# Remainder rows stacked by split half, and a masked broadcast of the running maximum by matmuls

## The chip, the cores and the metric

One core of a Trainium2 chip. The metric is the device time of one execution in microseconds, the median of several runs; lower is better.

## The reference

The input goes through three layers, all in 32-bit floats.

1. A recurrent attention (an mLSTM) over 2 batches, 8 heads, 768 positions and head size 40. With gates i and f, a running maximum m and a state C (40 x 40 per head):

```
m_new = max(f_t + m, i_t);  f_stab = exp(f_t + m - m_new);  i_stab = exp(i_t - m_new)
C = f_stab C + i_stab v_t k_t^T;   n = f_stab n + i_stab k_t
y_t = sigmoid(o_t) * (C q_t) / max(|n . q_t|, 1)
```

2. The 1536 tokens of 320 numbers are normalised (root mean square, times rms_g), then `silu(x w_gate) * (x w_val) @ w_out` with 1536 inner columns.
3. `leaky_relu(x w_in, 0.01) @ w_out` with 2048 inner columns.

## The kernel before, in words

**Attention.** The 768 positions are cut into 6 chunks of 128; chunk c of batch b is tile T = 2c + b, so there are 12 tiles. Within a tile the recurrence is written as a masked product: a cumulative sum Fl of f, a = i - Fl, and the running maximum A of a (both by scans on DVE over 16 rows, one per batch and head: `scan_f`, `scan_a`). The weight of position s for position t is exp(a_s - A_t) for s <= t. So each tile needs A_t as a row that all 128 partitions see. For tile 0 that is done by `first_a` (token `fa`): matmuls with one column of the identity, repeated 128 times, as weights and the 16 rows of A as moving data (L216), which leaves A in PSUM. For all other tiles A is stored to DRAM (`a_out`, L237) and loaded back to all 128 partitions (`ld_a`, token `da`, L274, 512 KB each). The causal mask adds 1e30 where s > t: on DVE inside `att_arg` for tiles 0 and 1 (L306, eight instructions per tile, then one wide exp per half on ACT, L310), on POOL for the rest (`att_mask`, L314), followed by four exps per half on ACT (L304). A half is the even or the odd heads (e = 0 or 1).

The further steps of a tile are `qk` (scores, L288), `p` (scores times weights, DVE), `av` (times v, by halves, L353), `inn` (product with the state of earlier chunks, L364), `k` and `kv` (keys times their weight, product for the state, L376), then the gating, the norm and `xn`, and `tp` (three transposes, L458). `xh` and `xl` write X, the normalised tokens with features on partitions, as two halves of a 32-bit number: the high half is what the format fp32r keeps, the low half is the rest.

**Weights.** Weights arrive as 64-bit floats and are turned into 32-bit ones by integer steps on DVE and ACT (`to_f32`), then split into high and low halves. The 320 features are 128 + 128 + 64. The main block of an up weight is token `a`; the 64 remaining rows of two blocks are loaded as one 128-partition block, token `r` (L523, L525), and their high and low halves are re-copied by DMA from SBUF to SBUF to both partition halves of their place, token `x` (`rest`, L531, two transfers of 128 KB per weight block).

**Up and down.** `up` forms each 128-column block in eight matmuls: high x high, high x low, low x high for the two full blocks, and for the 64 rows one matmul with the high weights and one with the low weights, in which partitions 64 to 127 of X hold the low half of the same 64 features. Token `U.g.f.h` is one such block (h = 0 gate, 1 value) of the second layer over a group of 3 or 4 tiles, `D` and `DW` its down products, `H` and `O` those of the third layer.

**Filling matmuls.** `busy` (token `id.1`, L182) multiplies constants of 512 columns in bf16; the result is not used. The order has 77 of them, 62 ahead of the first U and 15 behind it, of which six are at the very end.

**What sets the order.** The whole program is played from one string, ORDER: each token calls one function, and each engine executes its instructions in the order in which they were issued. All loads and stores are on the queue of SP, in that order too. Nothing is reordered later; an engine waits at an instruction until its data are there and its buffer is free.

Of the kernel before, what the change touches and what calls it, by code (L numbers as in the profile page):

```python
# [48 lines left out]
id.1 y2.0.0 co.1.1.2 a.0 cv.1.1.2 co.0.1.2 cv.0.1.2 qk.1 p.1.0 dc.1.2 co.0.2.6 dv.1.2 st.0 y2.0.1 y2.0.2 qk.2 da.2
mask.2.1 arg.2.1 p.1.1 k.2 r.1 id.1 dr.2.6 r.1 cb.0 a.0 dgb av.1.0 av.1.1 de.2 dE.2.6 wA.1 x.0 a.1 mask.2.0 a.2 xn.0  # L50
xc.0 a.1 a.1 x.1 id.1 dq.4 cv.0.2.6 a.2 id.1 tp.0 arg.2.0 abs.1 a.1 wR.2 y1.1 r.2 da.4 mask.4.0 id.1 id.1 rec.1 yr.1
a.2 wR.3 sq.1 id.1 a.2 r.2 xh.0 id.1 id.1 k.1 wA.3 a.3 kv.1 st.1 co.1.2.6 p.2.0 id.1 av.2.0 da.3 de.3 mask.3.0 arg.3.0
dq.3 r.2 p.2.1 av.2.1 xl.0 qk.3 cb.1 mask.3.1 id.1 eq.2 inn.2 cv.1.2.6 id.1 id.1 arg.3.1 wR.4 id.1 y2.1.0 y2.1.1
y2.1.2 a.3 r.2 a.3 id.1 x.2 id.1 id.1 xn.1 mask.4.1 wA.4 a.4 p.3.1 y1.2 dn.3 k.3 p.3.0 id.1 a.3 arg.4.1 abs.2 rec.2
qk.4 x.3 kv.2 id.1 de.4 eq.4 xc.1 tp.1 dn.4 arg.4.0 p.4.0 av.4.0 id.1 c.3 c.2 r.3 a.4 a.4 yr.2 eq.3 id.1 wA.5 da.5
mask.5.0 r.3 de.5 id.1 av.3.0 av.3.1 a.4 sq.2 y2.2.0 th.4 p.4.1 y2.2.1 r.3 dn.5 r.3 a.5 y2.2.2 xn.2 xc.2 id.1 mask.5.1
xh.1 id.1 id.1 inn.3 th.3 a.5 wR.5 abs.3 id.1 kv.3 y1.3 id.1 id.1 xl.1 tp.2 xh.2 xl.2 arg.5.0 id.1 dq.5 wA.6 qk.5
rec.3 yr.3 a.5 a.5 U.0.0.0 arg.5.1 b.0 a.6 eq.5 st.3 cb.3 p.5.0 p.5.1 k.5 T.0.0 E.0.0 sq.3 da.6 mask.6.1 dc.2.6 dv.2.6
b.0 a.6 b.0 b.0 U.0.0.1 av.4.1 dq.6 inn.4 a.6 abs.4 wB.1 av.5.0 mask.6.0 arg.6.0 c.5 y2.3.0 y2.3.1 qk.6 y2.3.2 U.0.1.0
T.0.1 y1.4 M.0.0 rec.4 yr.4 sq.4 dn.7 b.1 av.5.1 a.6 c.4 arg.6.1 k.4 kv.4 xn.3 id.1 xc.3 b.1 id.1 y2.4.0 y2.4.1 inn.5  # L60
kv.5 abs.5 x.6 wA.7 a.7 th.5 st.4 p.6.1 E.0.1 de.6 st.5 da.7 id.1 p.6.0 mask.7.0 wB.3 tp.3 xh.3 xl.3 S.0.0 dn.6 de.7
dq.7 wB.2 y1.5 U.0.1.1 U.0.2.0 a.7 b.1 L.0.0 a.7 a.7 mask.7.1 arg.7.1 eq.6 av.6.0 id.1 dq.8 av.6.1 rec.5 yr.5 sq.5 b.3
b.1 b.2 arg.7.0 T.0.2 y2.5.0 dn.10 b.3 id.1 id.1 id.1 b.3 M.0.1 y2.5.1 y2.4.2 xn.4 xc.4 y2.5.2 xn.5 xc.5 x.5 E.0.2 b.3
da.8 da.9 qk.7 id.1 p.7.0 U.0.2.1 S.0.1 L.0.1 tp.5 xh.5 xl.5 cb.4 th.7 c.6 wA.8 p.7.1 U.0.3.0 T.0.3 E.0.3 M.0.2 inn.6
qk.8 abs.6 tp.4 k.7 xh.4 xl.4 th.6 y1.6 wA.10 U.0.3.1 k.6 M.0.3 S.0.3 L.0.3 x.7 U.1.0.0 T.1.0 rec.6 U.1.1.0 E.1.0
S.0.2 yr.6 mask.8.0 arg.8.0 b.2 b.2 kv.6 st.6 mask.8.1 wB.5 b.5 L.0.2 b.2 b.5 b.5 cb.6 U.1.0.1 wB.4 M.1.0 T.1.1 E.1.1
D.0.0.0 K.0.0.0 mask.9.1 b.4 b.4 b.4 sq.6 U.1.1.1 M.1.1 b.4 wB.6 b.6 c.8 y2.6.0 dq.9 y2.6.1 p.8.0 b.6 b.5 U.1.2.1
U.1.2.0 D.0.0.1 cb.5 c.7 arg.8.1 y2.6.2 xn.6 S.1.1 D.0.0.2 b.6 xc.6 tp.6 xh.6 xl.6 av.7.0 p.8.1 wB.7 av.7.1 K.0.0.2
dn.8 k.8 av.8.0 id.1 L.1.1 de.8 av.8.1 T.1.2 eq.7 E.1.2 M.1.2 S.1.2 L.1.2 eq.8 x.4 b.6 th.8 r.4 r.4 r.4 wR.8 r.4 inn.8
y1.8 U.1.3.0 T.1.3 K.0.0.1 U.1.3.1 E.1.3 abs.8 M.1.3 wB.9 inn.7 kv.7 kv.8 S.1.0 b.7 da.10 abs.7 arg.9.1 qk.9 y1.7  # L70
U.0.5.1 b.7 L.1.0 dn.9 b.7 U.0.4.0 rec.8 yr.8 mask.9.0 de.9 S.1.3 L.1.3 D.1.0.2 T.0.4 E.0.4 b.7 arg.9.0 p.9.0 U.0.4.1
sq.8 mask.10.1 st.7 D.1.0.0 cb.7 c.9 p.9.1 r.5 k.9 K.1.0.0 K.1.0.2 M.0.4 S.0.4 L.0.4 U.0.5.0 T.0.5 E.0.5 av.9.0
D.1.0.1 M.0.5 S.0.5 mask.10.0 arg.10.0 L.0.5 U.0.6.0 T.0.6 E.0.6 y2.8.0 y2.8.1 y2.8.2 U.0.6.1 a.8 M.0.6 S.0.6 eq.9
# [757 lines left out]
```

## Time and profile before

| | |
|---|---|
| median of 3 runs | 491.5 us (490.97 to 492.52) |
| span of the profiled execution | 488.2 us |
| PE busy | 468.6 us (96%), 2785 matmuls |
| DVE, ACT, POOL busy | 282.5, 224.9, 62.8 us |
| moved by DMA | 51.10 MB |
| mean granted TensorE clock | 0.965 of full |

The span is from the first to the last instruction of the profiled execution; the page gives no other time for it. PE is TensorE's matmuls, PEclk the granted clock, of which 1.00 is 2.4 GHz and 0.50 is 1.2 GHz; a mean between them is a window with both. Matmuls are pipelined, so the length of one is more than its share of PE's time; a row that merges several gives the time of all.

### The profile page before, as it was taken

Reading aid. Unit: us, or ns where it says so; the run is one execution under the profiler, and the core shown is the slowest. Engines: PE = TensorE matmul, PEld = TensorE weight load, DVE = VectorE, ACT = ScalarE, POOL = GpSimd, SP = SyncE. Lnnn points to the kernel's source line nnn. Section 1 sums busy time; section 2 is a strip of 40 time slices with the busy share of each in tenths; the row PEclk is TensorE's granted clock in tenths of the full one; section 3 lists DMA queues with packets and bytes.
Section 4 is the critical chain, followed back from the end, with each engine's and each line's share of the span. In section 5 each row is a group of like instructions: output and inputs, shape, how many; then the busy total and the mean of one; then the engine's idle time right before and its main releaser. Section 6 shows DMA issues by size and latency. Waiting matters only on the chain.

```text
span 488.2 us, 7459 instructions
## 1 busy us (share of the span) xinstructions
PE 468.6 (96%) x2785; PEld 415.0 (85%) x2785; DVE 282.5 (58%) x618; ACT 224.9 (46%) x525; POOL 62.8 (13%) x82
## 2 busy tenths in 40 slices
PE   7959699899999998999999999999999999999998
PEld 4537589799999998999988888888898898988987
DVE  7776888877557676887767666654432121232232
ACT  2556366575533614655533444665434342532150
POOL 3325743513321200000000000000000000000000
PEclk7975869999999999999999999999999999999999
DMA  7899996963910011736430410232000000010101
GB/s 279 283 300 279 276 284 174 280 198 88 257 69 0 1 44 31 213 113 186 149 97 1 120 55 0 62 104 72 0 2 0 1 1 1 0 42 0 68 0 55
DMA packets 36868, 51.10 MB, mean 105 GB/s; under 512 B 2800, under 2 KB 26272, under 8 KB 36832
## 3 DMA queue, kind: packets, MB, share of 16 engines
q1 hardware_dynamic: 36832, 50.62, 35.7%
q8 instruction: 22, 0.36, 0.3%
q14 instruction: 14, 0.11, 0.1%
HBM read 43.31 MB, written 2.06 MB: 93 GB/s over the span
## 4 chain that ended last, share of the span: by engine, by line
PE 79%; DVE 8%; DMA 5%; issue 3%; ACT 2%; POOL 1%; SPq 1%; POOLq 0%; DVEq 0%; ACTq 0%
PE h L569 18%; PE g L569 13%; PE v L569 12%; PE xa L632 7%; PE oa L704 6%; PE oa L702 6%; PE oa L703 6%; PE xw L650 4%; PE o L353 2%; DMA Ab<-A_d 2%; DMA raw_A<-wgv 2%; PE s L288 1%; PE o L364 1%; DMA wA<-rest 1%; PE o L376 1%
## 5 line engine op out<-in xcount | busy, mean ns | idle before, releaser
L569 PE MATMUL h<-X,wA 128*128 128x512 f32 x384 | 93.0, 395 | 0.0
L569 PEld LDWEIGHTS h<-X,wA 128*128 128x128 f32 x384 | 71.4, 188 | 15.6
L614 DVE TENSOR_TENSOR sl<-u,sh 128x512 fp32r<-128x512 f32 x48 | 32.4, 690 | 85.3 <-ACT sh L608 85.3
L569 PE MATMUL g<-X,wA 128*128 128x384 f32 (+1 forms) x352 | 75.0, 359 | 0.0
L569 PE MATMUL v<-X,wA 128*128 128x384 f32 (+1 forms) x352 | 74.1, 356 | 0.6 <-DVE th L602 0.6
L569 PEld LDWEIGHTS g<-X,wA 128*128 128x128 f32 x352 | 63.5, 191 | 5.1 <-ACT wA L514 0.2
L569 PEld LDWEIGHTS v<-X,wA 128*128 128x128 f32 x352 | 62.3, 188 | 5.8 <-DVE th L602 0.9
L689 ACT ACTIVATE u<-h 128x512 f32<-128x512 f32 x48 | 28.2, 597 | 75.4 <-PE h L569 57.8
L704 PE MATMUL oa<-wB,sl 128*128 128x320 f32 x192 | 59.4, 309 | 0.0
L703 PE MATMUL oa<-wB,sh 128*128 128x320 f32 x192 | 59.3, 309 | 0.0
L702 PE MATMUL oa<-wB,sh 128*128 128x320 f32 x192 | 59.3, 309 | 0.0
L632 PE MATMUL xa<-sh,wB 128*128 128x384 f32 x160 | 46.2, 339 | 0.0
L608 ACT CAST sh<-th 128x384 fp32r<-128x384 f32 (+1 forms) x44 | 23.6, 541 | 46.8 <-DVE th L602 39.3
L703 PEld LDWEIGHTS oa<-wB,sh 128*128 128x128 f32 x192 | 36.0, 188 | 1.0
L702 PEld LDWEIGHTS oa<-wB,sh 128*128 128x128 f32 x192 | 36.0, 188 | 0.9
L704 PEld LDWEIGHTS oa<-wB,sl 128*128 128x128 f32 x192 | 36.0, 188 | 0.3 <-DVE sl L614 0.3
L591 ACT ACTIVATE th<-g 128x384 f32<-128x384 f32 (+1 forms) x44 | 22.7, 518 | 27.6 <-PE g L569 20.3
L598 DVE SCALAR_TENSOR_TENSOR th<-th,g 128x384 f32<-128x384 f32 (+1 forms) x44 | 25.7, 587 | 14.8 <-ACT th L591 14.2
L614 DVE TENSOR_TENSOR sl<-th,sh 128x384 fp32r<-128x384 f32 (+1 forms) x44 | 27.0, 617 | 12.2 <-ACT sh L608 11.9
L608 ACT CAST sh<-u 128x512 fp32r<-128x512 f32 x48 | 29.0, 620 | 9.4 <-PE oa L703 7.3
L632 PE MATMUL xa<-sl,wB 128*128 128x384 f32 x96 | 32.4, 338 | 0.0
L182 PE MATMUL busy<-const-bfloat16-1.0 128*128 128x512 bf16 x77 | 27.6, 477 | 4.1 <-DVE aeu L208 3.4
(113 smaller groups left out, 672.2 us busy)
## 6 DMA issues: line engine op xcount, KB each, us to landing
raw_B<-wo SPq DMA_DIRECT2D x28, 320.0 KB, 3.4
raw_A<-wgv SPq DMA_DIRECT2D x12, 512.0 KB, 6.1
qkt<-qk SPq DMA_DIRECT2D x12, 512.0 KB, 6.0
nat<-nat SPq DMA_DIRECT2D x12, 484.0 KB, 6.6
Ab<-A_d SPq DMA_DIRECT2D x11, 512.0 KB, 6.4
wA<-rest SPq DMA_DIRECT2D x40, 128.0 KB, 4.5
raw_A<-wi SPq DMA_DIRECT2D x8, 512.0 KB, 4.3
eb<-e_d SPq DMA_DIRECT2D x20, 128.0 KB, 6.4
```

Source lines behind the costliest of these rows:

```text
L182: PE.matmul(dst, idle[0], idle[1][:, 0:dst.shape[1]], start=start, stop=start)
L569: PE.matmul(dst, a, x, start=(i == 0), stop=(i == len(seq) - 1))
L591: A.activation(th, u[0], AF.Tanh, scale=0.5)
L598: V.scalar_tensor_tensor(out=u["t"], in0=u["t"], scalar=1.0, in1=u[0], op0=ALU.add, op1=ALU.mult)
L608: A.copy(u["h"], u["t"])
L614: V.tensor_tensor(u["l"], u["t"], u["h"].bitcast(F32), op=ALU.subtract)
L632: PE.matmul(xa, w, x, start=(k == 0), stop=(k == len(seq) - 1))
L650: PE.matmul(xas["w", g, i], a, x, start=(f == NE and k == 0), stop=(f == NF - 1 and k == len(seq) - 1),)
L689: A.activation(t, u[0], AF.Prelu, alpha=0.01)
L702: PE.matmul(dst, sh[:, ts], wb[:, 0:DM], start=first, stop=False)
L703: PE.matmul(dst, sh[:, ts], wb[:, DM:], start=False, stop=False)
L704: PE.matmul(dst, sl[:, ts], wb[:, 0:DM], start=False, stop=last)
```

## The change

Five things, and a new ORDER.

- **Remainder rows.** The place of the 64 remaining rows of a weight block is one column block of 128 partitions, high half on one side and low half on the other, written there by ACT and DVE directly. The re-copies (token `x`) are gone. X gets a sixth block, the low half of its third block; the two remainder matmuls of `up` use the stacked weights with the third and the sixth block.
- **Broadcast by matmuls.** `fa` is now called for both halves of tiles 0 to 3. One matmul of the identity with the mask (both in fp32r, 512 columns) starts the sum in PSUM, four matmuls add A. For these tiles ACT reads A from PSUM in four exps per half; the loads `da` and the masks on POOL for tiles 2 and 3 and the subtractions on DVE for tiles 0 and 1 are gone. The mask value is 2^100.
- **Gate rows** live in x2, which is not needed before the down products, and not in five of the eight places for up weights.
- Clearing of two tiles moves from DVE to POOL. The identity and the mask are loaded as one and copied to fp32r (token `cr`, ACT, twice in the order).
- The low part of X is one subtraction where it was two; A in DRAM is laid out by chunk, so that a broadcast reads 4 KB in one piece.

```diff
-        for j in range(4):
-            bh = 2 * j + e
-            PE.matmul(A0[e][:, j * L:(j + 1) * L], ident[0:16, bh:bh + 1].to_broadcast([16, 128]), A_[:, 0], start=True, stop=True)
+    def rows_a(T, e):
+        c, b = divmod(T, B)
+        pa = st_[T].setdefault("A", {})[e] = psum(f"A{T}_{e}", "acc" if b else "gv", 2)
+        PE.matmul(pa.rearrange("p (j l) -> p j l", j=4), ident_r, mask_r.unsqueeze(1).to_broadcast([128, 4, L]), start=True, stop=False)
+        for j in range(4):
+            bh = b * H + 2 * j + e
+            PE.matmul(
+                pa[:, j * L:(j + 1) * L], ident[0:16, bh:bh + 1].to_broadcast([16, 128]), A_[:, c], start=False, stop=j == 3,
+            )
...
-            if c > 0:
-                A.activation(w[:, j], t["Ab"][:, h], AF.Exp, scale=-1.0, bias=col)
...
+            src = t["A"][e][:, j * L:(j + 1) * L] if T < NPA else t["Ab"][:, h]
+            A.activation(w[:, j], src, AF.Exp, scale=-1.0, bias=col)
...
+        halves = [(up_weights(2 * i + e), slice(64 * e, 64 * e + 64), slice(64 - 64 * e, 128 - 64 * e)) for e in range(2)]
+        for w, hi, lo in halves:
+            A.copy(w[hi, 4], x[hi])
         yield
-        V.tensor_tensor(r[:, 1], x, r[:, 0].bitcast(F32), op=ALU.subtract)
+        for w, hi, lo in halves:
+            V.tensor_tensor(w[lo, 4], x[hi], w[hi, 4].bitcast(F32), op=ALU.subtract)
         yield
-
-    def rest(key):
-        r, lo, w = WR[key // 2], 64 * (key % 2), WA[key]
-        for i in range(2):
-            Q.dma_start(out=w[64 * i:64 * i + 64, :, 2].bitcast(F32), in_=r[lo:lo + 64].bitcast(F32))
...
-            (w[:, 0, 2, ms], X[:, 2, cs]), (w[:, 1, 2, ms], X[:, 2, cs]),
+            (w[:, 4, ms], X[:, 2, cs]), (w[:, 4, ms], X[:, 5, cs]),
```

The order is too long to show. PE's tokens up to the sixth U, without the fillers (which are in the order before alone):

```
before: co.0.0.1 fa.0 fa.1 qk.0 co.1.0.1 av.0.0 av.0.1 kv.0 co.1.1.2 co.0.1.2 qk.1 dc.1.2 co.0.2.6 qk.2 av.1.0 av.1.1
 tp.0 kv.1 co.1.2.6 av.2.0 av.2.1 qk.3 inn.2 qk.4 kv.2 tp.1 av.4.0 av.3.0 av.3.1 inn.3 kv.3 tp.2 qk.5 U.0.0.0 dc.2.6
 U.0.0.1 av.4.1 inn.4 av.5.0 qk.6 U.0.1.0 av.5.1 kv.4 inn.5 kv.5 tp.3 U.0.1.1 U.0.2.0 av.6.0 av.6.1 qk.7 U.0.2.1
after: co.0.0.1 fa.0.1 fa.1.1 co.0.1.2 fa.0.0 qk.0 fa.1.0 co.1.0.1 qk.1 co.0.2.6 av.0.0 av.0.1 fa.2.0 kv.0 av.1.0 av.1.1
 co.1.2.6 qk.2 fa.2.1 fa.3.1 co.1.1.2 kv.1 fa.3.0 av.2.0 qk.3 av.2.1 inn.2 av.3.0 av.3.1 inn.3 kv.3 qk.4 kv.2 tp.0 tp.1
 tp.2 dc.1.2 qk.5 U.0.1.0 U.0.0.0 U.0.1.1 av.4.0 av.4.1 inn.4 dc.2.6 av.5.0 av.5.1 inn.5 qk.6 kv.5 U.0.0.1 U.0.2.0
 U.0.2.1
```

(`co` transposes columns of gates, one per chunk; `dc` is the decay.) The loads issued ahead of the first U, as tokens times their size on the page:

```
before, to the load of tile 5's q and k: wA 6 x 512, wR 6 x 256, wB 1 x 320, q and k 6 x 512, nat 6 x 484, da 5 x 512,
 de 4 x 128 x 2, re-copies 4 x 128 x 2, small ones about 500 (KB)
after, to de of tile 4: wA 6 x 512, wR 4 x 256, wB 2 x 320, q and k 6 x 512, nat 5 x 484, da 3 x 512, de 4 x 128 x 2,
 small ones about 500 (KB)
```

## Rows read from the trace of the kernel before

**Rows 1.** The page, busy us (share of the span) and instructions per engine.

```profile
PE 468.6 (96%) x2785; PEld 415.0 (85%) x2785; DVE 282.5 (58%) x618; ACT 224.9 (46%) x525; POOL 62.8 (13%) x82
```

**Rows 2.** The page, the span in 40 slices, in tenths.

```profile
PEclk7975869999999999999999999999999999999999
DMA  7899996963910011736430410232000000010101
```

**Rows 3.** Windows, sum over 0 to 72 us: busy us (instructions) per engine.

```profile
sum 72.00, PE 57.80 PEld 41.27 DVE 54.76 ACT 35.74 POOL 30.90; mean PE 0.80 PEld 0.57 DVE 0.76 ACT 0.50 POOL 0.43
```

**Rows 4.** Timeline of PE, 27 to 72 us: start us, us, line, out<-in, count.

```profile
63.26 2.08 PE L288 MATMUL s<-qkt 40*128 40x128 f32 x16
65.27 2.93 PE L569 MATMUL g<-X,wA 128*128 128x384 f32 x8
```

**Rows 5.** Chain that ended last: start us, us, what.

```profile
45.82 9.07 DMA Ab<-A_d
...
154.87 1.39 PE g L569 x8
```

**Rows 6.** The page, DMA: the main queue, then issues with KB and landing us.

```profile
q1 hardware_dynamic: 36832, 50.62, 35.7%
...
Ab<-A_d SPq DMA_DIRECT2D x11, 512.0 KB, 6.4
wA<-rest SPq DMA_DIRECT2D x40, 128.0 KB, 4.5
```

**Rows 7.** Timeline of PE, 98 to 192 us.

```profile
110.59 2.77 PE L353 MATMUL o<-nat,w 128*128 128x41 f32 x24
...
114.22 1.10 PE L364 MATMUL o<-Cbd,eb 104*128 104x82 f32 x8
```

**Rows 8.** Timeline of PE, 27 to 72 us, rows at the low clock.

```profile
30.67 0.59 PE L182 MATMUL busy<-const-bfloat16-1.0 128*128 128x512 bf16 x1 [3.36 <-DVE aeu L208]
31.05 0.85 PE L458 MATMUL tp<-ident,xn 128*128 128x128 f32 x3
...
37.23 0.41 PE L204 MATMUL pt<-ident,gt 16*128 16x16 f32 x4
...
38.40 3.61 PE L353 MATMUL o<-nat,w 128*128 128x41 f32 x16 [0.44 <-PE busy L182]
41.96 2.08 PE L288 MATMUL s<-qkt 40*128 40x128 f32 x16
...
44.37 1.84 PE L364 MATMUL o<-Cbd,eb 104*128 104x82 f32 x8
46.00 2.71 PE L182 MATMUL busy<-const-bfloat16-1.0 128*128 128x512 bf16 x7
...
60.22 1.08 PE L376 MATMUL o<-nat,Kt 128*64 128x41 f32 x16 [3.96 <-ACT sm L403]
```

**Rows 9.** Windows of 1 us: busy us per engine, then PEclk, DMA share, GB/s.

```profile
27.00:28.00 1.00, 0.31 (x2) 0.03 (x1) 0.00 (x0) 0.00 (x0) 0.00 (x0) 0.80 1.13 230
...
34.00:35.00 1.00, 0.03 (x1) 0.00 (x0) 1.00 (x2) 0.93 (x3) 0.57 (x1) 0.79 1.03 357
...
45.00:46.00 1.00, 1.00 (x6) 1.00 (x6) 1.00 (x4) 0.79 (x2) 0.00 (x0) 0.50 1.22 254
...
48.00:49.00 1.00, 1.00 (x9) 0.46 (x9) 0.96 (x3) 1.00 (x5) 1.00 (x2) 0.96 1.06 287
...
68.00:69.00 1.00, 1.00 (x5) 0.83 (x5) 0.93 (x3) 0.94 (x3) 0.00 (x0) 0.72 1.15 244
```

**Rows 10.** Timeline of PE, 0 to 27 us.

```profile
0.77 3.11 PE L182 MATMUL busy<-const-bfloat16-1.0 128*128 128x512 bf16 x7 [0.77 <-PEq L822]
...
4.29 2.05 PE L216 MATMUL A<-gt,ident 16*128 16x128 f32 x16
...
20.04 1.70 PE L182 MATMUL busy<-const-bfloat16-1.0 128*128 128x512 bf16 x7
```

**Rows 11.** Costliest groups of instructions, shapes apart: busy us, mean ns, idle before.

```profile
L304 ACT ACTIVATE w<-Ab,aeu 128x128 f32<-128x128 f32 x80 | 25.4, 390 | 4.0 <-POOL Ab L314 3.9
```

More of the change, by code (lines that the diff above doesn't have):

```diff
@@ L29 @@
 BIG = 1e30
+MASKED = 2.0 ** 100
 NE = 8
 NBL = 11
+NPA = 4
 SB = 5
@@ L49 @@
[L49 to L73, printed above, removed]
@@ new lines @@
+arg.1.0 ex.1.2 wA.0 r.1 dn.0 eg.2.6 dn.1 dA.2.6 co.1.0.1 cv.1.0.1 cl uv.1.2 th.1 ug.2.6 wR.2 qk.1 r.2 r.0 co.0.2.6
+cv.0.2.6 k.0 dn.2 av.0.0 p.1.0 av.0.1 abs.0 a.0 rec.0 th.0 y1.0 r.2 fa.2.0 a.0 a.0 da.4 mask.4.1 dq.2 yr.0 kv.0 st.0
+dq.5 av.1.0 p.1.1 av.1.1 y1.1 r.2 dsl dE.1.2 sq.0 ux.2.6 ex.2.6 r.2 mask.4.0 y2.0.0 a.0 wA.1 a.1 co.1.2.6 wA.2 abs.1
+rec.1 a.1 a.2 a.1 cb.0 yr.1 sq.1 y2.1.0 y2.0.1 y2.0.2 qk.2 da.5 mask.5.1 fa.2.1 a.2 k.1 fa.3.1 arg.4.1 de.2 eq.2
+dr.1.2 ux.1.2 co.1.1.2 arg.3.1 cv.1.1.2 kv.1 st.1 mask.5.0 cv.1.2.6 a.1 dgb arg.2.1 arg.2.0 p.2.1 p.2.0 xn.0 dn.5
@@ new lines @@
+U.0.1.1 xn.3 M.0.1 k.5 dn.6 st.3 av.4.0 av.4.1 inn.4 b.0 dc.2.6 a.5 av.5.0 av.5.1 E.0.0 dq.9 dv.2.6 y1.4 mask.6.0
+abs.4 S.0.1 rec.4 da.7 L.0.1 cb.3 c.5 dq.6 inn.5 a.5 a.5 wA.6 wB.2 qk.6 kv.5 b.0 b.0 a.6 yr.4 c.4 th.5 arg.6.1 a.6
+y1.5 abs.5 rec.5 sq.4 y2.4.0 U.0.0.1 y2.4.1 k.4 b.1 arg.6.0 U.0.2.0 M.0.0 S.0.0 yr.5 sq.5 p.6.1 b.1 y2.5.0 de.7 y2.5.1
+U.0.2.1 T.0.2 E.0.2 M.0.2 kv.4 st.4 p.6.0 U.0.3.1 st.5 y2.4.2 de.6 th.6 y2.5.2 xn.5 S.0.2 xc.3 tp.3 xh.3 xl.3 eq.6
+xn.4 dn.8 cb.4 c.6 av.6.0 av.6.1 wR.4 inn.6 b.1 b.1 xc.5 tp.5 xh.5 de.9 L.0.2 k.6 U.0.3.0 xl.5 xc.4 y1.6 T.0.3 E.0.3
@@ new lines @@
+st.8 wB.8 de.11 U.0.7.1 b.7 tp.6 T.0.7 E.0.7 M.0.7 b.7 U.1.4.0 L.0.6 arg.10.0 p.10.0 S.0.7 y2.8.2 st.9 xn.8 xh.6 L.0.7
+eq.10 T.1.4 U.1.4.1 cb.9 E.1.4 M.1.4 D.0.1.0 D.0.1.2 xn.7 K.0.1.2 xc.7 U.1.6.0 T.1.6 xl.6 xc.8 U.1.6.1 E.1.6 M.1.6
+mask.10.1 rec.9 arg.10.1 S.1.4 L.1.4 p.10.1 y1.9 U.1.5.1 U.1.5.0 yr.9 T.1.5 E.1.5 sq.9 D.0.1.1 dn.10 th.10 av.10.0
+M.1.5 y2.9.0 S.1.5 L.1.5 tp.8 mask.11.1 y2.9.1 xh.8 xl.8 y2.9.2 S.1.6 L.1.6 qk.11 U.1.7.0 tp.7 T.1.7 eq.11 U.1.7.1
+xh.7 p.11.0 K.0.1.1 E.1.7 xl.7 M.1.7 U.2.1.0 S.1.7 T.2.1 L.1.7 D.1.1.2 K.1.1.2 cb.8 U.2.1.1 D.1.1.1 K.1.1.1 dn.11
@@ L145, in psum @@
         return ps.tile([128, 512], F32, tag=tag, name=name, bufs=bufs)
-    ident = const.tile([128, 128], F32, name="ident")
-    mask = attc.tile([128, 128], F32, name="mask")
+    consts = attc.tile([128, 256], F32, name="consts")
+    consts_r = attc.tile([128, 256], F32R, name="consts_r")
+    ident, mask = consts[:, 0:128], consts[:, 128:256]
+    ident_r, mask_r = consts_r[:, 0:128], consts_r[:, 128:256]
     sel = const.tile([16, 136], F32, name="sel")
@@ L153, in body @@
     x2 = const.tile([128, NTILE, 3, L], F32, name="x2")
-    X = const.tile([128, 5, NTILE * L], F32R, name="X")
+    X = const.tile([128, 6, NTILE * L], F32R, name="X")
     idle = [nc.const_aps.tensor(1.0, [128, n], BF16) for n in (128, 512)]
@@ L160, in body @@
     Kt = [attc.tile([128, 4, 104], F32, name=f"Kt{b}") for b in range(2)]
-    gt = [wpool.tile([16, 2, NC, L], F32, tag="wA", name=f"gt{i}") for i in range(5)]
-    i_, f_ = gt[0][:, 0], gt[0][:, 1]
-    rst, d_ = gt[1][:, 0], gt[1][:, 1]
-    Fl, a_ = gt[2][:, 0], gt[2][:, 1]
-    A_, em = gt[3][:, 0], gt[3][:, 1]
-    um = gt[4][:, 0]
-    Mc = gt[4][:, 1, 0, 0:NC]
-    rG = gt[4][:, 1, 1, 0:8 * (NC - 1)].rearrange("p (j c) -> p j c", j=8)
+    gates = [x2[0:16].rearrange("p n k l -> p (n k l)")[:, n * S:(n + 1) * S] for n in range(6)]
+    i_, f_, rst, d_, Fl, A_ = (g.rearrange("p (c l) -> p c l", c=NC) for g in gates)
+    a_, um, em = i_, f_, rst
+    Mc = attc.tile([16, NC], F32, name="Mc")
+    rG = attc.tile([16, 8, NC - 1], F32, name="rG")
     fl2 = lambda t: t.rearrange("p c l -> p (c l)")
-    A_d = dram.tile([BH, NC, L], F32, name="A_d")
+    A_d = dram.tile([NC, BH, L], F32, name="A_d")
     mhalf = const.tile([128, 1], F32, name="mhalf")
@@ L236, in a_out @@
     def a_out(c0, c1):
-        Q.dma_start(out=A_d[:, c0:c1], in_=A_[:, c0:c1])
+        Q.dma_start(out=A_d[c0:c1].rearrange("c p l -> p c l"), in_=A_[:, c0:c1])
     def decay_rows(c0, c1):
@@ L273, in ld_a @@
         st_[T]["Ab"] = Ab = loads.tile([128, H, L], F32, tag="Ab", name=f"Ab{T}", bufs=2)
-        Q.dma_start(out=Ab, in_=A_v[b, c].partition_broadcast(128))
+        Q.dma_start(out=Ab.rearrange("p h l -> p (h l)"), in_=A_v[b, c].partition_broadcast(128))
     def ld_e(T):
@@ L726, in body @@
     ops = dict(
-        ms=memsets, cl=clear, sf=scan_f, sa=scan_a, id=busy, fa=first_a,
+        ms=memsets, cl=clear, sf=scan_f, sa=scan_a, id=busy, fa=rows_a,
         dfg=lambda: Q.dma_start(out=fl2(f_), in_=fg), dig=lambda: Q.dma_start(out=fl2(i_), in_=ig),
-        did=lambda: Q.dma_start(out=ident, in_=cst[:, 0:128]), dmk=lambda: Q.dma_start(out=mask, in_=cst[:, 128:256]),
+        did=lambda: Q.dma_start(out=consts, in_=cst), cr=lambda: A.copy(consts_r, consts),
         dsl=lambda: Q.dma_start(out=sel, in_=cst2), dgb=lambda: Q.dma_start(out=gb, in_=rg.partition_broadcast(128)),
@@ L793, in _layout @@
     cst[:, 0:128] = np.eye(128)
-    cst[:, 128:256] = np.where(s[:, None] <= s[None, :], 0.0, BIG)
+    cst[:, 128:256] = np.where(s[:, None] <= s[None, :], 0.0, MASKED)
     bh = np.arange(16)
```

158 lines of the change are left out of this document (76 added, 82 removed).

## The prediction

> **What bounds the kernel now.** I read the table of busy times first: PE is busy 468.6 us of the span of 488.2, no other engine over 282.5 [rows 1]. The strips in 40 slices then show two stages [rows 2]: from the seventh slice on (73 us) PEclk is 9, and in the first six slices of 12.2 us DMA is at 7 to 9 tenths while PEclk wanders between 5 and 9. The windows say the same of the first 72 us: PE was busy 57.80 of them, DVE 54.76 [rows 3]. So whatever moves no TensorE work is worth little after some 70 us, and the place to look is the time at which the first up matmul (token U) starts. In the timeline of PE that is 65.27 us [rows 4]. The chain of waits back from there holds transfers above all; the longest piece is 9.07 us for a broadcast of the running maximum [rows 5]. I therefore price the change as: shift of the first U, plus TensorE work that moves across it, plus waits that come or go behind it. The profiled execution's own time is the span, 488.2 us; the median of the runs, 491.5, lies 3.3 above it, and I carry that 3.3 unchanged.
>
> **The change part by part.**
>
> *Re-copies and broadcasts that go.* 40 re-copies of 128 KB and 3 of the 11 broadcasts of 512 KB: 6,656 KB of the 50.62 MB on the queue, with their 43 issues on SP [rows 6]. By the order's tokens and the sizes of the page, the loads ahead of the first U were 16,000 KB up to the last one PE needed (q and k of tile 5) and become 13,300 KB. That last load was used at 63.26 us [rows 4], so the queue moved 253 KB per us; at this rate 13,300 KB end at 52.5 us. This is the bound from below for the new first U, should the transfers decide.
>
> *Order made anew, without the 77 filling matmuls.* Ahead of the first U both orders have qk for tiles 0 to 5, av for 0 to 3, the state products of 0 to 3 and three transposed tiles; only one half of av for tile 4 moves behind it (2.77 us for three halves and more at full clock [rows 7]; one half is eight instructions, 0.9, I take +0.8). What changes is the clock at which this is done. From 38.40 to 46.00 us PE has attention matmuls nearly without a gap, one filler among them [rows 8]; the granted clock is still 0.50 in 45 to 46 us and rises in 48 to 49, after seven fillers from 46.00 [rows 8, 9]. It fell in 27 to 28 us, rose in 34 to 35, and rose again in 68 to 69 us, after the first U [rows 9]. The order after has no filler ahead of U, so I price its whole front at the low clock, 1.2 GHz.
>
> By the Trainium skill ("TensorE: Matmul & The Clock Gate", section "Why this matters for your kernels") steady matmul work without gaps brings the full clock; taken at its word the front would be warm and end with the transfers, at 52.5 us. The trace disagrees for this kind of work: 7.6 us of it, and 0.50 at their end.
>
> *PE's old work ahead of U at the low clock* [rows 8]: 6 qk at 2.08 = 12.5; 8 halves of av at 1.8 (3.61 for two) = 14.4; 2 products with the state at 1.84 = 3.7; 4 state products at 1.08 = 4.3; 3 transposed tiles at 0.85 = 2.6; 12 small transposes of gates (0.41 for four, up to twice that at the low clock) and the decay, 2.4. Sum 39.9.
>
> *The new broadcasts.* Eight calls instead of two, each of four matmuls of 16 rows (two instructions each) and one of 512 columns with the mask. The old pair is 16 instructions in 2.05 us, so 1.03 a call [rows 10]. That was at the low clock too: seven fillers just before it took 3.11 us, 0.44 each, against 2.71 for seven from 46.00 and 1.70 for seven at full clock [rows 8, 10]. The mask matmul is as long as one low filler, 0.40. 8 x 1.43 = 11.4 us, where it was 2.05; at full clock it would be half, the bound from below.
>
> PE can start these at about 5.5 us (an estimate: 4.29 [rows 10], and 1.2 for one load and one scan that now stand in front). 5.5 + 39.9 + 11.4 = 56.8 with no wait at all. Waits: before, PE idled 14.2 of the first 72 us [rows 3], and two gaps of 3.36 and 3.96 us [rows 8] make half of it. The bounds are 0 and 14.2. As the transfers are due by 52.5, I keep 4 us, somewhat over half of the rest: each broadcast pair is freed only when ACT has read it, and ACT now has the short exps of tiles 0 and 1 too. First U at 60.8, which is 4.5 earlier.
>
> *DVE, ACT, POOL.* DVE loses the 16 subtractions of tiles 0 and 1 and the clearing, ACT gets 16 short exps at 0.32 (25.4 us for 80 [rows 11]) for four wide ones, POOL loses 4 of 20 masks. The last two steps of each remainder block are paid twice, on 64 partitions each. DVE was busy 76% of the first 72 us [rows 3]; all this hides beside PE and shows only as waits, which are in the 4 us. If that cover is gone, the dearest is ACT: 5.1 us of exps in the front. Over the kernel the low parts of X cost one DVE instruction where they were two; behind 70 us, beside a full PE, that is nothing either way, bounds -1 and +1.
>
> *Behind the first U.* The nine fillers that are not at the very end go: 1.70 us for seven, so 2.2, some of it in gaps; bounds 0 and 2.2, I take -1.0. The last six stand beside the final copies and cost nothing. Two U may run before the clock rises instead of one: 2.93 us against 1.39 [rows 4, 5], so 0 to 1.5, I take +0.7. Then a new risk: behind its third U the order has four halves of av, two products with the state, a qk and a state product in a row, half of 14.8 us by the low-clock rows above, 7 us, and no filler. Rows 7 begin a stretch of such work in which the slice still reads 9 [rows 2]; the fall in 27 to 28 us came behind such work [rows 9]. The low stretch there lasted about 7 us, so a drop costs half of that, 3.4. Bounds 0 and 3.4; the rows speak both ways, I take the middle, +1.7.
>
> Sum: -4.5 + 0.8 - 1.0 + 0.7 + 1.7 = -2.3: a span of 485.9, a time of **489.2 us**.
>
> **The rivals.**
>
> *Warm front, paced by transfers* (0.20). First U at 52.5, 12.8 earlier: 491.5 - 12.8 + 0.8 - 1.0 and 0 to 2.4 = 478.5 to 480.9. For it: qk and the mask matmuls are dense, and several of them follow one another early on. Against it: the stretch at 0.50 had a qk in it [rows 8]. The page's rule named above leads here.
>
> *The clock is lost again behind the first U* (0.25), the slower side. One mechanism: the fillers are gone, and rows of attention products between 65 and 190 us drop the clock, 3.4 us a time. Without any drop the sum is 487.5; with n drops it is 487.5 + 3.4 n: from two on it is slower than before (494.3), three give 497.7, four 501.1. For it: the fall in 27 to 28 us. Against it: PEclk 9 from 73 us on in before [rows 2], with only nine fillers there.
>
> *The transfers were hidden anyway* (0.10): PE's queue, not DMA, set 65.27, and hand-overs stay at 7 to 9 us. The first U comes at 64 to 66 and the time is 492 at the middle, 490.5 to 493.
>
> **How the numbers follow.** The forecast holds 0.45 and spans 485 to 493 (waits of 0 to 7 us in the front, no drop or one). About 1.5 us, 0.3%, is what can be told from no change. Faster: the warm front, 0.20, and two thirds of the forecast, 0.30. Same: 0.10 of the forecast and the hidden case, 0.10. Slower: the drops, 0.25, and the end of the forecast, 0.05. The range 479 to 500 leaves out a part of the warm front and the cases of four drops or more.
>
> **What would show it.** Granted clock 0.50 from about 7 us to the first U; first U at 59 to 63 us; PE busy over 85% of that time; no 128 KB re-copies; DMA share under 0.9 in the last windows before U. A granted clock of 1.00 between 15 and 50 us, or a first U before 55, makes the forecast wrong towards faster; a clock under 0.95 in the windows from 75 to 190 us, towards slower. If PE idles more than 7 us ahead of the first U, the hand-overs were undersized.

## The result, and the profile after

The changed kernel takes **498.0 us** (median of 4 runs, 496.39 to 500.6) against 491.24 (490.47 to 492.52) for the kernel before: a ratio of 1.0143, 95% interval 1.0102 to 1.0183. It is slower by 6.8 us, where 489.2 had been forecast. The profiled execution has a span of 498.8 us, the longest of the four (the others: 496.3, 496.0, 494.6), so its rows hold some 2.6 us more than the median.

The page after: busy time of PE, the strips in 40 slices, the main queue. The first row answers to [rows 1], the strips to [rows 2], the queue to [rows 6].

```profile
PE 481.8 (97%) x2764; PEld 438.1 (88%) x2764; DVE 285.1 (57%) x593; ACT 230.6 (46%) x549; POOL 63.7 (13%) x82
...
PEclk9999995999997999999999999999999999999999
DMA  7667752561285001141322210021000010000011
...
q1 hardware_dynamic: 20656, 43.79, 27.1%
```

The re-copies and three broadcasts from DRAM are gone (50.62 MB became 43.79), and DMA no longer stands at 9 in the front. But PE has fewer instructions and is busy 13 us longer, and its clock falls in two places behind the front. Next the timeline of PE (start us, us, line, out<-in, count): the first two broadcasts, which answer to [rows 10], and the first U, which answers to [rows 4].

```profile
5.52 0.79 PE L212 MATMUL A<-consts_r 128*128 128x512 f32 x1 [0.34 <-ACT consts_r L723]
6.24 2.07 PE L215 MATMUL A<-x,consts 16*128 16x128 f32 x8
8.24 0.80 PE L212 MATMUL A<-consts_r 128*128 128x512 f32 x1
...
65.38 2.08 PE L289 MATMUL s<-qkt 40*128 40x128 f32 x16
67.39 4.43 PE L567 MATMUL g<-X,wA 128*128 128x384 f32 x16
```

Eight instructions take 2.07 us; before, sixteen took 2.05 [rows 10]. From the start of one mask matmul to the next is 2.72 us: the price of a broadcast, where I had 1.43. The first U is at 67.39, 2.1 later than before. Windows of the front (busy us of each engine, PEclk, DMA share, GB/s) show who sets this; the sum over 72 us answers to [rows 3].

```profile
10.00:30.00 20.00, 20.00 (x111) 17.39 (x110) 11.30 (x27) 10.98 (x35) 7.79 (x11) 1.00 0.59 209
30.00:50.00 20.00, 19.75 (x108) 17.01 (x107) 16.02 (x33) 12.10 (x38) 11.30 (x12) 1.00 0.83 256
...
sum 72.00, PE 64.62 PEld 56.45 DVE 46.29 ACT 36.30 POOL 26.04; mean PE 12.92 PEld 11.29 DVE 9.26 ACT 7.26 POOL 5.21
```

PE has no gap from 10 to 30 us and 0.25 us of gaps from 30 to 50: the front is bound by TensorE, not by transfers. The column PEclk says 1.00 here, yet qk takes 2.08 us, as in the low rows of before [rows 8], and no instruction has its full-clock length before 71 us. In this trace the column reads full until the fall at 77 us; the first change in its record is a rise at 70 us, and nothing is recorded ahead of that. Durations have to be trusted over it.

Behind the first U, 431.4 us follow, where 422.9 did; PE was busy 421.8 and 417.6 of them, so half of the difference is longer busy time and half is waiting. Five windows there, and one of the kernel before:

```profile
75.00:80.00 5.00, 4.44 (x27) 4.15 (x27) 4.34 (x11) 1.46 (x5) 0.67 (x2) 0.73 0.33 100
80.00:85.00 5.00, 5.00 (x41) 4.55 (x42) 2.78 (x7) 2.85 (x9) 0.61 (x2) 0.50 0.25 72
85.00:90.00 5.00, 5.00 (x23) 5.00 (x23) 3.47 (x11) 3.94 (x13) 1.66 (x4) 0.75 0.71 205
...
100.00:110.00 10.00, 8.29 (x59) 7.52 (x54) 8.50 (x19) 5.37 (x18) 3.90 (x4) 1.00 0.79 270
110.00:120.00 10.00, 8.64 (x49) 8.32 (x49) 7.87 (x9) 6.04 (x16) 8.90 (x11) 1.00 0.17 57
```
```profile
100.00:120.00 20.00, 20.00 (x162) 19.81 (x160) 14.20 (x38) 12.37 (x39) 6.57 (x8) 1.00 0.51 146
```

From 77 to 87 us the clock is low: it falls within the row of attention products behind the third U, after two halves of av, a product with the state and 0.4 us of waiting. (A second low stretch lies between 149 and 156 us, behind a transfer of q and k on which PE waited 1.1 us.) And from 100 to 120 us PE stands still for 3.1 us with a full clock, where before it was busy 20.00 of 20.00. The waits in that stretch, in the timelines of PE, DVE and POOL:

```profile
109.39 0.62 PE L630 MATMUL xa<-sh,wB 128*128 128x384 f32 x2 [1.71 <-DVE wB L539]
116.86 1.66 PE L567 MATMUL v<-X,wA 128*128 128x384 f32 x8 [1.35 <-DVE th L596]
```
```profile
106.20 1.73 DVE L517 TENSOR_TENSOR wA<-w_A,wA 128x512 fp32r<-128x512 f32 x1 [0.35 <-ACT wA L515]
...
109.39 0.54 DVE L612 TENSOR_TENSOR sl<-th,sh 128x384 fp32r<-128x384 f32 x1
...
111.57 4.12 DVE L612 TENSOR_TENSOR sl<-th,sh 128x384 fp32r<-128x384 f32 x1 [0.44 <-ACT sh L606]
```
```profile
106.10 2.95 POOL L309 TENSOR_TENSOR Ab<-Ab,consts 128x512 f32<-128x512 f32 x2 [8.97 <-DMA Ab<-A_d]
...
111.47 1.29 POOL L309 TENSOR_TENSOR Ab<-Ab,consts 128x512 f32<-128x512 f32 x1
112.72 2.54 POOL L313 TENSOR_TENSOR eb<-eb,qkt 128x512 f32<-128x512 f32 x2
```

The same subtraction takes 0.54 us and, beside GpSimd's mask and gate products, 4.12; in the kernel before none between 65 and 200 us takes more than 1.28.

So there are two losses: 2.1 us in the front and some 5 behind it. My first theory was the clock: without fillers the front runs at 1.2 GHz and the rows behind drop it. The rivals were the price of the broadcasts themselves, the new order, and later GpSimd beside VectorE.

### The profile page after: what moved, and what is told of

It is laid out like the page before. It is cut to its first block, busy times and chain, and to the rows that moved or that the text cites. A ratio compares the mean times of both kernels' runs of the same rounds, so it can differ in the third digit from the quotient of the medians.

```text
span 498.8 us, 7343 instructions
## 1 busy us (share of the span) xinstructions
PE 481.8 (97%) x2764; PEld 438.1 (88%) x2764; DVE 285.1 (57%) x593; ACT 230.6 (46%) x549; POOL 63.7 (13%) x82
## 3 DMA queue, kind: packets, MB, share of 16 engines
q1 hardware_dynamic: 20656, 43.79, 27.1%
## 4 chain that ended last, share of the span: by engine, by line
PE 86%; DVE 7%; ACT 3%; DMA 2%; issue 1%; SPq 0%; DVEq 0%; ACTq 0%
PE h L567 18%; PE v L567 11%; PE g L567 11%; PE xa L630 8%; PE oa L696 6%; PE oa L697 6%; PE oa L698 6%; PE o L348 4%; PE xw L648 4%; PE s L289 4%; PE A L215 3%; DMA qkt<-qk 2%; PE o L359 2%; PE o L371 1%; PE A L212 1%
## 5 line engine op out<-in xcount | busy, mean ns | idle before, releaser
L567 PE MATMUL v<-X,wA 128*128 128x384 f32 (+1 forms) x352 | 76.3, 363 | 1.4 <-DVE th L596 1.4
L567 PEld LDWEIGHTS v<-X,wA 128*128 128x128 f32 x352 | 64.6, 194 | 6.4 <-DVE th L596 2.0
L630 PE MATMUL xa<-sh,wB 128*128 128x384 f32 x160 | 45.1, 338 | 1.7 <-DVE wB L539 1.7
L612 DVE TENSOR_TENSOR sl<-th,sh 128x384 fp32r<-128x384 f32 (+1 forms) x44 | 29.4, 673 | 10.4 <-ACT sh L606 10.0
L348 PEld LDWEIGHTS o<-nat,w 128*128 128x128 f32 x192 | 30.5, 245 | 1.1 <-issue 0.7
```

The costliest lines, as they stand in the source:

```text
L348: PE.matmul(num[:, 2 * p + e], t["w"][e][:, p, :], t["vn"][:, 2 * p + e, :], start=(c == 0 or (e == 0 and p == 0)), stop=c == 0,)
L567: PE.matmul(dst, a, x, start=(i == 0), stop=(i == len(seq) - 1))
L612: V.tensor_tensor(u["l"], u["t"], u["h"].bitcast(F32), op=ALU.subtract)
L630: PE.matmul(xa, w, x, start=(k == 0), stop=(k == len(seq) - 1))
```

## Experiments

Each was timed against the kernel before on the same chip. "Filler" is the token `id.1`. First U and the part behind it are from the profiled execution.

### The kernel before without its fillers

```diff
-id.1 dfg id.1 id.1 id.1 ms dig id.1 id.1 sf.0.1 sa.0.1
+dfg ms dig sf.0.1 sa.0.1
...
```

> The kernel before, with its order and all its parts, only the 77 filling matmuls taken out. Clock theory (without fillers TensorE stays at 1.2 GHz until the first up matmul and falls back in long rows of attention products): the first U moves from 65.3 to between 67 and 73 us, the clock is lost once or twice behind it, and the time is 494 to 503 us. Rival, the new order or the broadcasts make the whole loss and fillers only fill idle time: 490 to 493 us. If fillers stood in the way of work: 485 to 489.

492.29 us, ratio 1.0029 (1.0005 to 1.0053). The first U comes 0.9 us earlier (64.39), the part behind takes 2.6 more. All 77 fillers together were worth about 1.4 us; their loss alone is no explanation. The run also has the old pair of broadcasts, the sixteen instructions of [rows 10], with no filler ahead of them:

```profile
4.05 3.78 PE L213 MATMUL A<-gt,ident 16*128 16x128 f32 x16 [0.20 <-DVE gt L191]
```

They take 3.78 us here and 2.05 behind the fillers.

### Fillers put into the new order: ahead of the first U, and ahead and behind

```diff
-wR.0 dfg dig ms
+id.1 id.1 id.1 id.1 id.1 id.1 id.1 id.1 id.1 id.1 wR.0 dfg dig ms
...
-av.4.0 av.4.1 inn.4
+av.4.0 id.1 av.4.1 id.1 id.1 inn.4
```

(57 ahead in the first kernel; 57 and 18 in the second, which has the lower hunk.)

> The changed kernel with 57 filling matmuls put back ahead of the first U alone (10 at the start, one or two behind most of PE's tokens). Clock theory: the front runs at full clock, qk takes 1.16 us and not 2.08, a broadcast 1.4 and not 2.75, the first U comes at 52 to 58 us where it was 67.4, the two drops behind it stay, and the time is 484 to 489 us. Rival, the front is held by hand-overs of the new order and not by PE's rate: first U at 64 to 68, time 495 to 500.

> As front_fill, and 18 more fillers in the two rows of attention products behind the first U in which the changed kernel lost the clock (tiles 4 to 6 and tile 9). Clock theory: no window at 0.50 behind 60 us, 5 to 10 us less than front_fill, 476 to 484 us. Rival, those stretches wait for DVE and transfers anyway: within 2 us of front_fill.

508.92 us (ratio 1.0357, 1.0306 to 1.0408) and 506.46 (1.0292, 1.0259 to 1.0326). The fillers, ten at the start and then one or two at a time, brought the full clock to the first broadcast (its eight instructions take 1.15 us) and then not before 72 us. Windows of the front of the first, and its first U:

```profile
10.00:30.00 20.00, 19.94 (x89) 13.99 (x88) 9.05 (x23) 8.27 (x28) 7.78 (x11) 0.50 0.50 181
30.00:50.00 20.00, 19.69 (x106) 14.26 (x105) 10.59 (x26) 8.99 (x27) 6.32 (x6) 0.50 0.60 180
50.00:70.00 20.00, 19.94 (x87) 16.07 (x86) 10.62 (x25) 8.54 (x28) 4.68 (x6) 0.50 0.66 215
```
```profile
80.13 2.19 PE L570 MATMUL g<-X,wA 128*128 128x384 f32 x11
```

The recorded clock is 0.50 for 60 us in which PE is busy over 98% of the time. Here the Trainium skill ("TensorE: Matmul & The Clock Gate", section "Why this matters for your kernels"), by which gapless matmul work brings the full clock, is contradicted for this mix of short matmuls and fillers. What this front would take at the full clock stays unmeasured. In the order before, fillers lay in PE's waits; here PE has few waits, so most of them is paid: the first U comes 12.7 us later, and 10.7 in the second kernel, which has the same 57 ahead (first U at 78.05).

### The parts of the change in the old order

```diff
-x.10
+r.4 r.4 r.4 r.4
...
-NPA = 4
+NPA = 1
```

The changed functions, played by the order before with its fillers; only tile 0 is broadcast by matmuls.

> The changed kernel's functions played in the order of before, with its 77 fillers: stacked remainder rows, no re-copies, gate rows in x2, but the broadcast by matmuls for tile 0 alone (tile 1 is loaded and masked on POOL); some remainder steps stand later, where their place is free. If the transfers held the front: first U at 56 to 62 us, 482 to 488 us. If they were hidden: 489 to 493. If the parts themselves cost (remainder steps paid twice on ACT and DVE): 494 to 499.

491.76 us, ratio 1.0005 (0.9979 to 1.0031), first U at 65.46. The removed re-copies, the stacked remainder and the gate rows in x2 are worth nothing either way, although 5 MB less go over the queue. The loss is in the six added broadcasts or in the new order.

### The old order with tiles 0 to 3 broadcast, with and without fillers

```diff
-NPA = 1
+NPA = 4
...
-da.3 de.3 mask.3.0 arg.3.0
+de.3 fa.3.0 arg.3.0
```

> The old order with its 77 fillers and the parts of the change, as in the run in which only tile 0 was broadcast (491.8 us), but now with tiles 0 to 3 broadcast and masked by matmuls and without the fetches and GpSimd masks of tiles 1 to 3. Theory A (a broadcast is work like any other: six more are 6 x 1.43 = 8.6 us at full clock and 6 x 2.75 = 16.5 at the low one; the old front has some 9 us of idle TensorE that can hide a part): first up-projection at 67 to 72 instead of 65.5, 494 to 499 us. Rival B (broadcasts are free and the new order is the whole loss): first up-projection at 63 to 66, 488 to 492 us.

> The old order with tiles 0 to 3 broadcast and masked by matmuls, now without its 77 fillers. Theory A (the loss in the front is the broadcasts' work at the low clock, whatever the order): the front's work is the same as in the changed kernel, about 63 us at the low clock, so the first up-projection is at 66 to 70 us instead of 77.9 with fillers, and the time 492 to 498. Rival B (the old order also needs its waits of some 9 us in the front): first up-projection at 72 to 76, 498 to 504.

506.21 us (ratio 1.0303, 1.0259 to 1.0347), first U at 77.86; without fillers 505.98 (1.0318, 1.0283 to 1.0354), first U at 77.16. The first went further than theory A's numbers, the second even a little beyond rival B's: old order and matmul broadcasts do not go together, fillers or not. Without fillers in both, the first U moves from 64.39 to 77.16: the six broadcasts cost 12.8 us there. PE's busy time up to the first U rises from 45.48 to 62.56 us, by 17.1, so its waits hid only 4.3 of the new work, and 14.6 us of waits remain. The changed kernel does the same at 67.39, so the new order gives back 9.8 of them. In the run with fillers one broadcast is seen at either clock (timeline of PE):

```profile
7.13 0.80 PE L215 MATMUL A<-consts_r 128*128 128x512 f32 x1
7.86 2.07 PE L218 MATMUL A<-x,consts 16*128 16x128 f32 x8
...
17.34 0.58 PE L215 MATMUL A<-consts_r 128*128 128x512 f32 x1
17.86 1.15 PE L218 MATMUL A<-x,consts 16*128 16x128 f32 x8
```

2.07 us low, 1.15 full: the old pair, 2.05 us for both [rows 10], ran at the full clock, and at 3.78 without fillers at the low one.

### Fillers behind the first U alone

The lower hunk of the fillers' diff, in the changed kernel.

> The changed kernel with 18 filler matmuls put into the attention rows behind the first up-projection, and none ahead of it. Theory A (of the 10.6 us lost, some 5 to 6 are the two stretches at half clock behind the first up-projection; with fillers behind and ahead the part behind it took 425.0 us against 431.4): first up-projection unchanged at 67.4, no stretch at 0.50 behind it, 491 to 494 us. Rival B (half a clock costs no more there than the fillers' own 18 x 0.34 = 6.1 us): 497 to 501.

495.66 us, ratio 1.0095 (1.0061 to 1.0129): 2.3 us better than the changed kernel, about half of what theory A had, and the intervals of the two overlap. In the profiled execution the clock still fell twice (0.50 from 80 to 85 us, 0.83 from 110 to 120), and it took 497.83 us; the other three, with a mean recorded clock of 1.00, took 495.33 to 495.90. So the fillers kept the clock up in three executions of four, and both falls together cost some 2.4 us.

### Tiles 2 and 3 fetched again, in the new order

```diff
-NPA = 4
+NPA = 2
...
-av.0.0 p.1.0
+da.2 mask.2.1 mask.2.0 av.0.0 p.1.0
```

> The changed kernel with only tiles 0 and 1 broadcast by matmuls; tiles 2 and 3 are fetched from DRAM and masked on GpSimd as before, everything else and the order stay. Theory A (the front of the changed kernel is one row of TensorE work, and each broadcast is 2.75 us of it at the low clock): four broadcasts less are 11.0 us less; some 1 to 3 us come back as waits, so the first up-projection is at 57 to 60 us instead of 67.4, and the time is 487 to 491 us. Rival B (the new order is what is late: transfers or VectorE stand right behind TensorE in the front): the first up-projection stays at 64 to 68 us and the time at 494 to 499. Rival C (the two clock falls behind the first up-projection are the whole loss of 8.5 us there, and they grow when the front gets shorter): first up-projection at 57 to 60, but the time at 493 to 498.

> Both at once: tiles 2 and 3 fetched as before and 18 fillers behind the first up-projection. Theory A: first up-projection at 57 to 60, no half clock behind it, 482 to 486 us, under the kernel before (491). If the two effects are not additive (the clock falls for other reasons once the front is shorter): 487 to 492. Rival B (the order is late whatever is taken out): 494 or more.

508.29 us (ratio 1.0358, 1.0328 to 1.0388), first U at 74.45; with the fillers behind, 503.38 (1.0267, 1.0230 to 1.0304). Four broadcasts less, and slower. The edit does more than was expected of it: it also gives the maxima a third buffer and moves the fetch of tile 5's maximum. I had put that fetch ahead of other head loads, and it waited on SP's queue for a buffer, as the timelines of SP and PE show.

```profile
30.64 0.59 SPq L724 DMA_DIRECT2D gb<-rg  x1
43.23 0.33 SPq L275 DMA_DIRECT2D Ab<-A_d  x1
43.66 0.38 SPq L268 DMA_DIRECT2D nat<-nat  x1
```
```profile
52.77 2.08 PE L289 MATMUL s<-qkt 40*128 40x128 f32 x16 [6.88 <-DMA qkt<-qk]
```

So these two say nothing on broadcasts; the next pair moves that fetch.

```diff
-arg.2.0 da.5 mask.5.1 mask.5.0 p.2.1
+arg.2.0 p.2.1
...
-dn.3 av.3.0
+dn.3 da.5 mask.5.1 mask.5.0 av.3.0
```

> The run with tiles 2 and 3 fetched instead of broadcast, with the fetch and mask of tile 5 moved behind the head loads of tiles 2 and 3 on SP's queue, so that its wait for a buffer (11.9 us there) holds none of them up. Theory A (four broadcasts are 11 us of TensorE in the front, and the transfers fit when no wait blocks their queue): the 10 us of waits (3.0 and 6.9) are gone and the first up-projection is at 60 to 65 us instead of 74.5 and 67.4; the time is 490 to 496. Rival B (the fetches fill the queues whatever their order, so the broadcasts bought their price back in transfers): first up-projection at 67 to 73, 498 to 505.

> The same with the 18 fillers behind the first up-projection. Theory A: 2 to 4 us under the run without them, 487 to 493 us, which would be at or under the kernel before (491). Rival B: 495 to 502.

500.49 us (ratio 1.0211, 1.0161 to 1.0260), first U at 67.58; with fillers behind 496.60 (1.0143, 1.0091 to 1.0195). Rival B, at its edge. PE is busy 49.73 us up to the first U, where the changed kernel has 60.0, and yet the first U stays where it was. The waits on the way:

```profile
39.80 0.28 PE L202 MATMUL pt<-consts,x 16*128 16x16 f32 x1 [5.20 <-DVE rG L242]
40.01 1.07 PE L371 MATMUL o<-nat,Kt 128*64 128x41 f32 x16
44.07 1.90 PE L348 MATMUL o<-nat,w 128*128 128x41 f32 x8 [2.99 <-issue]
```

What the broadcasts leave, waits take: 5.2 us on VectorE's queue and 3.0 that the profile shows no releaser for. Right behind TensorE stands a second chain, about equally long. In the chain that ended last no transfer and no mask stands behind 5 us; from 24.9 to 39.8 us it runs for the most part over VectorE: the tile's steps and the weights' conversion. So here it is VectorE's queue that takes TensorE's place; that the fetches fill the queues, as rival B had it, is not shown.

### A cheaper broadcast

```diff
-    ident[0:16, bh:bh + 1].to_broadcast([16, 128]), A_[:, c], start=False, stop=j == 3,
+    ident_r[0:16, bh:bh + 1].to_broadcast([16, 128]), half[:, c],
...
+        V.tensor_copy(Ah[:, c], A_[:, c])
+        V.tensor_tensor(Al[:, c], A_[:, c], Ah[:, c], op=ALU.subtract)
```

> The changed kernel with the maximum's rows of the first two chunks split by VectorE into a rounded part and a rest (two small operations for each chunk), so that a broadcast is 4 pairs of fp32r matmuls of 16x128 instead of 4 fp32 ones of the same shape; order, mask matmuls and transfers stay. Theory A (the front is one row of TensorE work, so what a broadcast gives up comes off the time): by a quarter of the mask matmul's 0.72 us for 512 columns, a 128-column fp32r matmul is 0.11 to 0.18 us, eight of them 0.9 to 1.4 us instead of 2.0, eight broadcasts 5 to 9 us less: first up-projection at 59 to 63 instead of 67.4, 489 to 493 us. Rival B (transfers or VectorE are right behind TensorE in the front): first up-projection at 65 to 68, 495 to 499. Rival C (an fp32r matmul of 128 columns takes as long as one pass of an fp32 one, 0.26 us): nothing changes, 497 to 500.

> The split broadcasts and the 18 fillers behind the first up-projection together. Theory A: the two gains add, 5 to 9 us from the front and 2.3 from the fillers (measured before: 498.0 to 495.7): 486.5 to 490.5 us, under the kernel before (491). Rival B as for the split alone: 493 to 496. Rival C: 495 to 497.

497.14 us (ratio 1.0135, 1.0099 to 1.0171), first U at 66.67; with fillers behind 495.51 (1.0108, 1.0070 to 1.0146). Rival C, nearly: in the timeline of PE, `Ah` is the rounded part and `Al` the rest.

```profile
9.12 0.41 PE L222 MATMUL A<-Al,consts_r 16*128 16x128 f32 x1
9.34 0.41 PE L222 MATMUL A<-Ah,consts_r 16*128 16x128 f32 x1
9.55 0.41 PE L222 MATMUL A<-Al,consts_r 16*128 16x128 f32 x1
```

They start 0.21 us apart, against 2.07 / 8 = 0.26 for a pass of the fp32 form. From one mask matmul's start to the next (5.49 to 8.12 us) a broadcast takes 2.63 us instead of 2.72; eight of them are the 0.7 us by which the first U is earlier. My quarter of a 512-column matmul, 0.18, was too low as a price for 128 columns.

### Without GpSimd's masks of tiles 4 to 11

```diff
-mask.4.1 dq.2
+dq.2
...
```

All 16 mask tokens are left out; those tiles are not masked.

> The changed kernel without the 16 additions of the causal mask that GpSimd makes on the fetched maxima of tiles 4 to 11 (left out altogether, so those tiles are not masked); order, transfers and everything else stay. Theory D (GpSimd's additions hold up VectorE's two-operand instructions, one of 4.1 us at 111.6 us, and TensorE waits 1.7 and 1.4 us for them): the longest such instruction in 104 to 120 us falls to under 2 us, the two waits of TensorE there go, and the time falls by 2 to 4 us, to 494 to 496. Rival E (the long instruction has another cause, or GpSimd's other work takes the masks' place): the waits stay within 1 us, 497 to 499 us.

492.42 us, ratio 1.0050 (1.0006 to 1.0094): 4.6 us better than the changed kernel by the ratios, more than theory D had. The first U is at 67.42 as before, so all of it lies behind. The windows that PE waited in:

```profile
100.00:110.00 10.00, 9.03 (x50) 8.29 (x49) 7.20 (x15) 6.46 (x19) 4.88 (x5) 1.00 0.75 270
110.00:120.00 10.00, 10.00 (x71) 9.92 (x71) 6.27 (x13) 6.58 (x18) 2.35 (x5) 1.00 0.16 52
```

The group of VectorE's subtraction from 67 to 200 us (busy us, mean ns), first in the changed kernel, then here:

```profile
L612 DVE TENSOR_TENSOR sl<-th,sh 128x384 fp32r<-128x384 f32 x20 | 14.6, 732 | 3.8 <-ACT sh L606 3.7
```
```profile
L611 DVE TENSOR_TENSOR sl<-th,sh 128x384 fp32r<-128x384 f32 x20 | 11.0, 553 | 3.9 <-ACT sh L605 3.9
```

The same 20 instructions take 3.6 us less, and the second low stretch is gone as well. By the Trainium skill ("SBUF — State Buffer", section "SBUF: two separate sides") VectorE and GpSimd share one pair of ports, and a VectorE instruction with two inputs in SBUF that comes second to a GpSimd instruction reading SBUF is blocked for the whole of that instruction. The 4.12 us agree with a block, but with one that lasts over three GpSimd instructions of 1.3 us in a row. In the run without masks the same subtraction took 0.62 us at 108.91, within a row of two GpSimd instructions, the second of which starts at 109.1 (timelines of DVE and POOL):

```profile
108.91 0.62 DVE L611 TENSOR_TENSOR sl<-th,sh 128x384 fp32r<-128x384 f32 x1 [0.45 <-ACT sh L605]
```
```profile
107.83 2.86 POOL L312 TENSOR_TENSOR eb<-eb,qkt 128x512 f32<-128x512 f32 x2 [1.10 <-DMA raw_B<-wo]
```

So it came in at the border between the two. What lets it in at one border and holds it over two others stays open, as does how much of the 4.6 us is the ports and how much the second fall of the clock, which came in the one profile and not in the other. The fall is hardly the main part: with a mean recorded clock of 0.989 or 0.990 the changed kernel took 497.88 and 498.13 us, this one 491.62 to 492.50 in five executions and 495.04 in a sixth. (Two more of this one, at 0.982 and 0.983, took 498.21 and 497.52, so a further fall may cost as much as the masks.)

None of the fourteen beats the kernel before.

## Why the prediction was wrong, step by step

**What bounds the kernel.** "The chain of waits back from there holds transfers above all": true of before, and without consequence. 5 MB fewer transfers in the old order moved nothing (ratio 1.0005). The third rival, transfers hidden anyway, was right on this point, though not in its time, as it left out the broadcasts.

**Low clock in the front: right.** The old work ahead of U, priced at 39.9 us, took about 38: 67.39 less the start at 5.52, eight broadcasts of 2.72 and 2.0 of gaps behind the start. The start, forecast at 5.5, was exact; the waits were 2.0, not 4. PE was busy 60.0 of 67.39 us, 89%, over the 85% I had asked for.

**The new broadcasts: the step that failed.** "That was at the low clock too", I wrote of the 2.05 us for sixteen instructions [rows 10], since seven fillers just before took 3.11. But the fillers that start this program were no gauge for the rows behind them: by the time of the broadcasts the clock was up. Without fillers ahead of them the same sixteen take 3.78 us, and eight of them take 1.15 or 2.07 us at the two clocks. In the kernel before, the clock's record begins with a rise at 3.7 us, and the windows in which the broadcasts ran, from 4.29 to 6.34 us, read 1.00 (the third number from the end):

```profile
4.00:5.00 1.00, 1.00 (x8) 0.77 (x8) 0.93 (x5) 0.00 (x0) 0.00 (x0) 1.00 0.81 299
5.00:6.00 1.00, 1.00 (x11) 1.00 (x11) 1.00 (x2) 0.00 (x0) 0.00 (x0) 1.00 1.00 377
```

The other half of the term, "The mask matmul is as long as one low filler, 0.40", was off by nearly the same factor, but not for the clock: at the low clock it takes 0.72 us from its start to the next instruction, for as many columns in fp32r as the filler has in bf16. 8 x 1.43 = 11.4 us was in fact 8 x 2.72 = 21.8. That is +10.4; with -2.0 for the waits and -1.8 for the old work it makes the +6.6 between 60.8 and 67.39. I had named half of 11.4, the full clock, as the only other bound, so the range of this term did not reach upwards at all. Of the 8.8 us between forecast and result these 6.6 are the larger part.

**"All this hides beside PE": wrong behind the first U.** I had DVE and POOL only as work in the front. The new order puts ten GpSimd instructions into 106 to 116 us, and VectorE, which has the up products' split to make there, is held up by them. The masks cost the changed kernel 4.6 us (measured by leaving them out), and with the 2.1 us of the front that comes to the 6.8. That their new place is the cause of all of it is not shown: the kernel before makes the same 16 masks, and it was not run without them. For the place speaks that PE idles 5.4 us behind the first U before, 9.6 in the changed kernel and 5.0 without the masks. Part of the same time is the clock's: fillers that mostly kept it up brought 2.3 us with the masks in place, so the two do not simply add.

**Fillers and the clock behind U.** I had -1.0, +0.7 and half a drop, +1.7. Two drops came in the profiled execution, as in the slower rival from n = 2 on. Its mechanism did occur, but its time for three drops (497.7) is near the measured one by luck. Its price was too high: in three kernels with the 18 fillers behind U (in the changed kernel, with the split broadcasts, and with the later fetches) the one execution whose mean recorded clock was 0.989 or 0.990 took 2.4 to 3.4 us more than the others, for all its falls together. The 18 fillers brought 2.3 us in the changed kernel and 1.6 to 4.9 in the others. And the rival's base, 487.5, contained the broadcasts at half their price. The row of products that was named for the risk adds up to 14.1 us by [rows 8], not 14.8; its half, 7, stands.

**The warm front** did not come; nothing in the trace had spoken for it but a page's rule.

**What had been named as a sign** "towards slower", a clock under 0.95 from 75 to 190 us, was there (0.82 from 72 to 100 us). Granted clock 0.50 from 7 us on cannot be read from the column, but from the durations. PE idling over 7 us ahead of U was 7.4 with the 4.9 at the start, not hand-overs.

## What to carry to other kernels

Before a duration is carried to new work, find out at which clock it was taken, from the same instruction at either clock and not from a neighbour, and keep the other clock as a bound on both sides. Moving work from DMA and GpSimd to TensorE pays only where it fits into TensorE's waits: in the old order six broadcasts cost 12.8 us, though 18.9 us of waits stood ahead of the first U, and an order that hid most of that left the engine 2 us of waits behind its start, so that fillers, cheap before, cost 10.7 to 12.7. When GpSimd's work is moved in time, look at which two-operand VectorE instructions it now runs beside.
